# RWKV attention with an ELU feed-forward: one three-bank PSUM tile becomes a two-bank tile and a one-bank tile

## The chip, the cores and the metric

The kernel runs on one core of a Trainium2 chip. The metric is device time in microseconds (us) of one execution. The engines are named as the profile names them: PE is TensorE's matmul side, PEld its weight loads, DVE is VectorE, ACT is ScalarE, POOL is GpSimd, SP is SyncE, whose queue issues nearly all loads.

## The reference

A linear attention with a decaying state, followed by a feed-forward layer. Everything is float32: 4 batches, 8 heads, 768 steps, head width 48; the feed-forward goes from 384 to 2048 and back.

```python
state = np.zeros((B, H, D, D))
for t in range(S):
    kt, vt, rt, wt = k[:, :, t], v[:, :, t], r[:, :, t], w[:, :, t]
    cur = np.einsum('bhd,bhe->bhde', u[None] * kt, vt)
    y[:, :, t] = np.einsum('bhd,bhde->bhe', rt, state + cur)
    state = wt[:, :, :, None] * state + np.einsum('bhd,bhe->bhde', kt, vt)
...
x = y.transpose(0, 2, 1, 3).reshape(B * S, H * D)
h = x @ w_in
g = np.where(h > 0.0, h, np.exp(np.minimum(h, 0.0)) - 1.0)
return g @ w_out
```

## The kernel before

The 768 steps are cut into 24 attention units. Units 0 to 3 each take one batch's first 128 steps ("whole" units); units 4 to 23 each take 64 steps of two batches. From unit 8 on a unit is "stacked": the inter-chunk and intra-chunk parts of an output share one matmul operand. The feed-forward runs in six chunks of 512 tokens (four units each) over 16 slices f of the inner width.

A unit goes through these steps. DVE scans the decay (`es`, `gs`) and scales k and r with it (`rh`). The diagonal term is made by PE and copied out by ACT in units 0 to 3 (`pd`, `md`), later by DVE, and then spread into a masked matrix `am` (`sp`: ACT in units 0 to 3, DVE in 4 to 7, POOL from 8 on). PE transposes k (`tr`), ACT copies the result out (`kt`). PE makes the scores (`s`), and DVE merges them into `am` under the causal mask (`mk`, lines 625 to 631). PE then makes the unit's outputs and the state update (`v`). ACT rounds the outputs to a high part (`xh`, line 692; in whole units by way of a plain copy `xf`, line 699), DVE makes the low part (`xl`, line 696), and DVE adds the update to the state (`up`, line 704; ACT at line 706 in whole units). In stacked units the step `v` of unit i issues three things in a row on PE: the scores of unit i+1, the state update of unit i, and the outputs of unit i.

In the feed-forward, each slice is nine matmuls into a tile `ph` (`g1`, line 303; three in line 299 while a chunk's weights are still plain float32), two ACT passes (`r1`, `r2`, lines 307 and 310), a DVE pass (`stt`, line 313), a split into high and low by ACT (`gh`, line 317) and DVE (`gl`, line 321), and nine matmuls into three accumulators (`g2`, lines 334 and 331). The weights arrive raw and are converted by ACT and DVE during the first 160 us (lines 719 to 753).

PSUM holds eight banks: three accumulators, two `ph`, and the tile `px` of three banks, made once at line 409 and used for the whole run. Banks 0 and 1 of it take the scores and the state update, and, in units 0 and 2 to 7, the outputs too. Unit 1 borrows two accumulators. Bank 2, reached through `single()` at line 445, takes the diagonal sums, the transposes, the outputs of stacked units (line 672) and a small check. In the last chunk the final output block is summed in two column pieces: columns 0 to 383 in bank 0 of `px` and columns 384 to 511 in bank 2 (lines 902 and 903); DVE adds a partial sum to each (line 348).

A planner in the kernel (`Plan`, with costs, due times and hand-fitted nudges) works out the order of all steps once, and they are emitted in that order: each engine works its own steps strictly in it. The planner takes no account of which tile a PSUM bank belongs to. The waits between engines are not written in the kernel: the framework derives them from which instructions touch which tile. A fixed number of filler matmuls into an accumulator (`warm`) stands ahead of some PE steps of the first 28 us.

Of the kernel before, what the change touches and what calls it, by code (L numbers as in the profile page):

```python
# [8 lines left out]
F32 = mybir.dt.float32  # L9
# [11 lines left out]
P = 128  # L21
# [5 lines left out]
NK = DM // P  # L27
N = B * C
GT = 4
L = C // 2  # L30
# [334 lines left out]
def rwkv_elu_kernel(ctx, tc, wkr, rk, vp, u, uz, gkrw, gv, gu, wraw, out):  # L365
# [16 lines left out]
    ps_a = pool("ps_a", 1, space=PS)  # L382
# [23 lines left out]
    xf = wide[:, 0:NK * N].rearrange("p (k n) -> p k n", k=NK)  # L406
    stack = wide.rearrange("p (s h n) -> p s h n", s=3, h=2)
    ams = cst.tile([P, 2, 2 * NP * C], F32, name="ams")
    px = ps_a.tile([P, 3, N], F32, name="px")
    sv = st[:, :, :, 16:16 + D]  # L410
    units = [dict(c=i // B, i=i, whole=i < B, last=i >= NU - STEP, L=C if i < B else L,
                  b=slice(i, i + 1) if i < B else slice(2 * (i % STEP), 2 * (i % STEP) + 2)) for i in range(NU)]
# [30 lines left out]
        return [px[:, q] for q in range(2)] if u_["whole"] else px[:, 0:2]  # L443

    def single():
        return px[:, 2]

    def spare():
        if not held:
# [73 lines left out]
    def diag_pe(u_):  # L523
        u_["pd"] = pd = single()[:, 0:NS].rearrange("t (p z) -> t p z", p=NP)
        for p in range(NP):
            nc.tensor.matmul(pd[:, p], u_["rkc"][:, p, :], ubd[:, p, :], start=True, stop=True)
# [47 lines left out]
    def job(u_, h, p, x, l, r, **flags):  # L574
        k, j = divmod(3 * p + (0, 1, 1, 2)[x], 4)
        nc.tensor.matmul(u_["py"][32 * j:32 * j + 32, h, k], l, r, **flags)  # L576
# [9 lines left out]
    def transposes(u_):  # L586
        u_["pt"] = pt = single()[:, 0:NP * R2].rearrange("t (p d) -> t p d", p=NP)
        for p in range(NP):
            nc.tensor.transpose(pt[:, p], u_["k"][:, p, :], ident[0:R2, 0:R2])

    def scores(u_, pa, each=False, close=True):
        for p in range(NP):
            for lo in range(0, C, u_["L"]):
                for q in range(2):
                    rs, ts = slice(64 * q, 64 * q + D), slice(lo, lo + u_["L"])
                    nc.tensor.matmul(pa[q][ts, p], u_["k"][rs, p, ts], u_["r"][rs, p, ts], start=each or p == 0, stop=each or (close and p == NP - 1))  # L596

    def halves():
        t = px[:, 0:2, 0:NP * L].rearrange("t q (p s) -> t q p s", p=NP)
        return [t[:, q] for q in range(2)]  # L600
# [40 lines left out]
    def update_part(u_, v, **flags):  # L641
        rows = [slice(0, C)] if u_["whole"] else [slice(L * h, L * h + L) for h in range(2)]
        for p in range(NP):
            for z in range(2):
                lo = 64 * z
                for h, rs in enumerate(rows):
                    nc.tensor.matmul(u_["pu"][lo:lo + D, h, p], u_["kt"][rs, p, lo:lo + D], v[h][rs, P * p + 80 * z:P * p + 80 * z + D],  # L647
                                     **{n: x if isinstance(x, bool) else p == x for n, x in flags.items()})
# [15 lines left out]
    def stacked(u_):  # L664
        i, w = u_["i"], u_["stack"]
        ahead = i + 1 < NU
        if ahead:
            scores(units[i + 1], halves(), close=u_["last"])
        if not u_["last"]:
            u_["pu"] = px[0:R2, 0:2, NP * L:NP * L + NP * D].rearrange("d h (p e) -> d h p e", p=NP)  # L670
            update_part(u_, [w[:, h] for h in range(2)], start=False, stop=NP - 1)
        u_["py"] = px[:, 2, 0:2 * NK * L].rearrange("d (h k t) -> d h k t", h=2, k=NK)
        for h in range(2):
            rs = slice(0, P if h else R2)
            for n, (p, x) in enumerate(VALUES):
                job(u_, h, p, x, w[rs, h, P * p + 32 * x:P * p + 32 * x + 32], u_["am"][rs, h, x // 2, p],
                    start=(h == 0 and n < 4), stop=(h == 1 and n >= len(VALUES) - 4))
# [82 lines left out]
    def guard():  # L760
        units[0]["pf"] = pf = single()[0:1, 0:NU + 1]
        nc.tensor.matmul(pf, ones_c, flags, start=True, stop=True)
# [105 lines left out]
    for c in range(NC):  # L868
        fns = mlp(nc, w_h, w_l, ps_acc, ps_h, ml, gp, stg, out[:, c * N:(c + 1) * N], last=c == NC - 1, w_f=() if c else w_f)
        t = BEGINS[c]  # L870
# [244 lines left out]
```

## Time and profile before

| | |
|---|---|
| median of 3 runs | 509.65 us |
| lowest, highest | 508.42, 514.08 us |
| profiled execution, device time | 512.53 us |
| profiled execution, span from first to last instruction | 510.7 us |
| PE busy in the span | 492.8 us (96%) |
| DVE, ACT, POOL busy | 350.3, 271.0, 42.0 us |
| mean granted TensorE clock | 0.990 |

The profiled execution has 1.8 us around its span. Times in the rows below are microseconds from the start of that span. A row of the timeline gives start, duration, engine, line of the kernel, operation, written tile <- read tiles, shape and count, and in brackets how long the engine sat idle before it and what ended that. A tile name has no bank: `px` stands for all three.

### The profile page before, as it was taken

To read this page: it belongs to the slowest core of one execution; us is meant where nothing else is said; L and a number is where in the kernel's file an instruction comes from. 1 tells how busy PE (TensorE), PEld (TensorE's weight loads), DVE (VectorE), ACT (ScalarE), POOL (GpSimd) and SP (SyncE) were. 2 spreads that over 40 slices of the span, in tenths; PEclk is the share of its full clock that TensorE was granted. 3 is DMA by queue.
4 is the path that set the end of the run, shared out by engine and by line. 5 is a ranking of instruction groups with operands and counts; after the bars stand their busy time and mean duration, and the time that the engine had idled before them with its cause. 6 is when DMAs were issued, how large, how long until landed. Compare 5 with 4: busy or idle time off the path is not lost.

```text
span 510.7 us, 12038 instructions
## 1 busy us (share of the span) xinstructions
PE 492.8 (96%) x5014; PEld 404.7 (79%) x5014; DVE 350.3 (69%) x525; ACT 271.0 (53%) x526; POOL 42.0 (8%) x57
## 2 busy tenths in 40 slices
PE   8997999999999999998999999999999999999994
PEld 8896887777887888886887777877888878888883
DVE  7899899989998998544898554599564352323432
ACT  4796568755764544635655525437445253634451
POOL 2000000002234011020011020020101000000000
PEclk9898999999999999999999999999999999999998
DMA  8999246734625444433951427033340100010001
GB/s 280 336 270 286 69 142 198 231 115 125 183 49 125 130 117 104 125 91 88 238 154 53 138 64 195 21 103 84 95 109 11 24 2 0 20 45 0 1 0 65
DMA packets 45611, 57.27 MB, mean 112 GB/s; under 512 B 29168, under 2 KB 29296, under 8 KB 45552
## 3 DMA queue, kind: packets, MB, share of 16 engines
q1 hardware_dynamic: 45120, 55.66, 39.0%
q8 instruction: 41, 0.67, 0.6%
q10 hardware_dynamic: 432, 0.79, 0.4%
q14 instruction: 18, 0.15, 0.1%
HBM read 45.42 MB, written 4.72 MB: 98 GB/s over the span
## 4 chain that ended last, share of the span: by engine, by line
PE 67%; DVE 17%; DMA 7%; issue 3%; ACT 3%; SPq 2%; DVEq 0%; ACTq 0%
PE ph L303 27%; PE acc L334 25%; PE px L576 3%; PE acc L331 3%; PE ph L299 3%; DMA wx<-in_wkr_dram 3%; DMA wraw<-in_wraw_dram 2%; DVE m L313 2%; DVE gl L321 2%; DVE k L502 2%; DVE eg L487 2%; DMA k<-in_wkr_dram 2%; PE px L596 2%; DVE ams L631 1%; PE px L647 1%
## 5 line engine op out<-in xcount | busy, mean ns | idle before, releaser
L313 DVE SCALAR_TENSOR_TENSOR m<-m,ph 128x512 f32<-128x512 f32 (+2 forms) x104 | 66.5, 641 | 72.0 <-ACT m L310 71.9
L303 PE MATMUL ph<-xh,w_l 128*128 128x512 f32 x270 | 105.5, 391 | 0.8 <-DVE w_l L753 0.8
L334 PE MATMUL acc<-gh,w_l 128*128 128x512 f32 x268 | 104.6, 390 | 0.0
L307 ACT ACTIVATE m<-ph 128x512 f32<-128x512 f32 (+2 forms) x104 | 58.5, 563 | 78.8 <-PE ph L303 60.0
L321 DVE TENSOR_TENSOR gl<-m,gh 128x512 fp32r<-128x512 f32 x90 | 62.1, 691 | 41.5 <-ACT gh L317 41.4
L317 ACT CAST gh<-m 128x512 fp32r<-128x512 f32 x90 | 55.5, 617 | 59.4 <-PE acc L334 36.6
L303 PE MATMUL ph<-xh,w_h 128*128 128x512 f32 x180 | 72.2, 401 | 1.5 <-DVE m L313 1.4
L334 PE MATMUL acc<-gl,w_h 128*128 128x512 f32 x180 | 70.6, 392 | 1.4 <-DVE gl L321 1.4
L334 PE MATMUL acc<-gh,w_h 128*128 128x512 f32 x180 | 71.7, 398 | 0.0
L303 PE MATMUL ph<-xl,w_h 128*128 128x512 f32 x180 | 70.2, 390 | 0.0
L310 ACT ACTIVATE m<-m 128x512 f32<-128x512 f32 (+2 forms) x104 | 62.1, 599 | 2.1
L303 PEld LDWEIGHTS ph<-xh,w_l 128*128 128x128 f32 x270 | 50.7, 188 | 12.1 <-DVE w_l L753 1.2
L334 PEld LDWEIGHTS acc<-gh,w_l 128*128 128x128 f32 x268 | 50.3, 188 | 10.3
L555 POOL TENSOR_SCALAR_AFFINE_SELECT ams<-md 64x512 f32<-64x512 f32 x32 | 29.1, 909 | 217.8 <-PE px L576 145.5
L303 PEld LDWEIGHTS ph<-xh,w_h 128*128 128x128 f32 x180 | 33.8, 188 | 9.7 <-DVE m L313 2.1
L334 PEld LDWEIGHTS acc<-gl,w_h 128*128 128x128 f32 x180 | 33.8, 188 | 9.6 <-DVE gl L321 3.1
L334 PEld LDWEIGHTS acc<-gh,w_h 128*128 128x128 f32 x180 | 33.8, 188 | 8.0 <-ACT gh L317 0.4
L303 PEld LDWEIGHTS ph<-xl,w_h 128*128 128x128 f32 x180 | 33.8, 188 | 6.5
L303 PE MATMUL ph<-xh,w_g 128*128 128x512 f32 x90 | 35.6, 395 | 0.1
L334 PE MATMUL acc<-gh,w_g 128*128 128x512 f32 x88 | 34.9, 397 | 0.7 <-ACT gh L317 0.7
L487 DVE TENSOR_TENSOR_SCAN eg<-w,reset 112x520 f32<-112x520 f32 (+1 forms) x24 | 30.7, 1278 | 6.6 <-DMA w<-in_wkr_dram 6.6
L303 PE MATMUL ph<-xl,w_g 128*128 128x512 f32 x90 | 35.1, 390 | 0.0
(110 smaller groups left out, 691.9 us busy)
## 6 DMA issues: line engine op xcount, KB each, us to landing
wraw<-in_wraw_dram SPq DMA_DIRECT2D x16, 768.0 KB, 10.1
k<-in_wkr_dram SPq DMA_DIRECT2D x24, 448.0 KB, 5.4
rk<-in_rk_dram SPq DMA_DIRECT2D x20, 384.0 KB, 4.4
w<-in_wkr_dram SPq DMA_DIRECT2D x24, 227.9 KB, 3.9
wide<-in_vp_dram SPq DMA_DIRECT2D x32, 128.0 KB, 3.5
out_dram<-o SPq DMA_DIRECT2D x15, 256.0 KB, 2.5
ams<-k SPq DMA_DIRECT2D x64, 48.0 KB, 2.6
wide<-st SPq DMA_DIRECT2D x64, 48.0 KB, 2.1
```

The costliest lines, as they stand in the source:

```text
L299: nc.tensor.matmul(ph, w_f[f][:, 0, k], x_[2][:, k], start=(k == 0), stop=(k == NK - 1))
L303: nc.tensor.matmul(ph, w[f][:, 0, k], y[:, k], start=(k == n == 0), stop=(k == NK - 1 and n == 2))
L307: act(s["m"], s["ph"], AF.Relu, scale=-1.0)
L310: act(s["m"], s["m"], AF.Exp, scale=-1.0)
L313: stt_(s["m"], s["m"], -1.0, s["ph"], ALU.add, ALU.max)
L317: nc.scalar.copy(s["gh"], s["m"])
L321: nc.vector.tensor_tensor(s["gl"], s["m"], s["gh"].bitcast(F32), ALU.subtract)
L331: nc.tensor.matmul(a_, w_f[f][:, 1, m], fold(s, s["m"][:, a:b]), start=first, stop=final)
L334: nc.tensor.matmul(a_, w[f][:, 1, m], fold(s, g[:, a:b]), start=(first and n == 0), stop=(final and n == 2))
L487: nc.vector.tensor_tensor_scan(out=eg[:, 0, 0:n][:, ::-1], data0=u_["w"][:, 1:n + 1][:, ::-1], data1=reset[:, 0, 0:n][:, ::-1], initial=0. ...
L555: nc.gpsimd.affine_select(out=am[rs, h].rearrange("t q p s -> t (q p) s"), in_=u_["md"][rs].rearrange("t q p -> t (q p)").unsqueeze(2).bro ...
L576: nc.tensor.matmul(u_["py"][32 * j:32 * j + 32, h, k], l, r, **flags)
```

## The change

The tile of three banks is made as two tiles: `px` with banks 0 and 1, `py` with one bank. What used `px[:, 2]` uses `py`. No step, shape, operand order or planner entry is different.

```diff
-    px = ps_a.tile([P, 3, N], F32, name="px")
+    px = ps_a.tile([P, 2, N], F32, name="px")
+    py = ps_a.tile([P, N], F32, name="py")
...
     def single():
-        return px[:, 2]
+        return py
...
-        u_["py"] = px[:, 2, 0:2 * NK * L].rearrange("d (h k t) -> d h k t", h=2, k=NK)
+        u_["py"] = py[:, 0:2 * NK * L].rearrange("d (h k t) -> d h k t", h=2, k=NK)
```

## Rows read from the trace of the kernel before

**Rows 1.** The page: busy time of the engines, and the chain that ended last.

```profile
PE 492.8 (96%) x5014; PEld 404.7 (79%) x5014; DVE 350.3 (69%) x525; ACT 271.0 (53%) x526; POOL 42.0 (8%) x57
...
PE 67%; DVE 17%; DMA 7%; issue 3%; ACT 3%; SPq 2%; DVEq 0%; ACTq 0%
```

**Rows 2.** Busy time by stretch: stretch, length, then each engine's busy time.

```profile
108.01:153.58 45.57, 44.58 (x646) 35.71 (x645) 45.34 (x66) 27.61 (x54) 11.76 (x11) 1.00 0.43 120
32.64:44.32 11.68, 10.45 (x109) 8.72 (x107) 11.64 (x17) 9.27 (x25) 1.07 (x2) 1.00 1.04 267
```

**Rows 3.** Timeline, PE: instructions before which PE sat idle.

```profile
14.44 1.05 PE L526 MATMUL px<-ubd,rkc 112*128 112x2 f32 x8 [1.22 <-ACT kt L635]
...
46.16 1.76 PE L576 MATMUL px<-ams,wide 128*32 128x128 f32 x32 [2.46 <-issue]
...
102.56 0.60 PE L589 MATMUL px<-ident,k 112*128 112x112 f32 x4 [0.37 <-DVE xl L696]
...
119.42 0.50 PE L303 MATMUL ph<-xh,w_l 128*128 128x512 f32 x1 [0.79 <-DVE w_l L753]
...
163.06 0.50 PE L303 MATMUL ph<-xh,w_h 128*128 128x512 f32 x1 [1.01 <-DVE m L313]
...
232.84 0.50 PE L334 MATMUL acc<-gl,w_h 128*128 128x512 f32 x1 [1.09 <-DVE gl L321]
...
270.15 0.51 PE L334 MATMUL acc<-gh,w_g 128*128 128x512 f32 x1 [0.69 <-ACT gh L317]
```

**Rows 4.** Waits: engine, line <- what ended them: total us, times, longest.

```profile
ACT xh L692 <- DVE ams L631: 25.0, 8, 6.8
...
DVE ams L631 <- PE px L576: 14.3, 5, 4.7
```

**Rows 5.** Timeline, 149 to 155 us: after the outputs of unit 8.

```profile
149.85 1.12 PE L576 MATMUL px<-ams,wide 112*32 112x64 f32 x64
...
152.09 1.49 DVE L631 COPY_PREDICATED ams<-upper_h,px 64x512 f32<-64x512 uint32 x2
...
153.67 0.48 ACT L692 CAST xh<-px 128x384 fp32r<-128x384 f32 x1 [1.60 <-DVE ams L631]
...
154.18 0.55 DVE L704 TENSOR_TENSOR st<-st,px 112x384 f32<-112x384 f32 x1 [0.60 <-ACT xh L692]
```

**Rows 6.** Timeline, 13 to 46 us, ACT and DVE around units 0, 2 and 3.

```profile
13.85 0.53 ACT L635 COPY kt<-px 128x448 f32<-128x448 f32 x1 [1.34 <-DVE ams L625]
...
32.64 1.35 DVE L625 COPY_PREDICATED ams<-upper,px 128x512 f32<-128x512 uint32 x2 [0.42 <-ACT kt L635]
...
42.54 0.71 ACT L310 ACTIVATE m<-m 128x256 f32<-128x256 f32 x2
...
43.91 0.41 DVE L313 SCALAR_TENSOR_TENSOR m<-m,ph 128x256 f32<-128x256 f32 x1
44.72 1.34 DVE L625 COPY_PREDICATED ams<-upper,px 128x512 f32<-128x512 uint32 x2 [0.39 <-ACT kt L635]
```

**Rows 7.** Timeline, DVE, 93 to 109 us.

```profile
93.85 0.75 DVE L627 COPY_PREDICATED ams<-upper_h,px 128x512 f32<-128x512 uint32 x1 [0.94 <-ACT kt L635]
...
108.01 0.96 DVE L753 TENSOR_TENSOR w_l<-wg,w_h 128x768 fp32r<-128x768 f32 x1 [2.08 <-ACT w_h L741]
```

**Rows 8.** Timeline from 502.9 us, then the chain's piece at 504.02.

```profile
502.96 0.34 PE L334 MATMUL px<-gh,w_l 128*128 128x384 f32 x1
...
504.02 0.76 DVE L348 TENSOR_TENSOR o<-px,part 128x384 f32<-128x384 f32 x2 [1.06 <-PE px L334]
...
504.02 0.56 DVE o L348
```

**Rows 9.** The chain that ended last, at 225 us.

```profile
225.78 3.49 DMA wx<-in_wkr_dram
```

**Rows 10.** Waits of PEld at the scores; timeline, PE, outputs of unit 9.

```profile
PEld px L596 <- issue: 4.6, 13, 0.4
...
160.95 1.10 PE L576 MATMUL px<-ams,wide 112*32 112x64 f32 x64
```

## The prediction

> **What bounds the kernel now.** I read the page first: PE is busy 492.8 of 510.7 us, and the chain that ended last runs through PE for 67% and DVE for 17% [rows 1]. So only what shortens PE's idle time, or the end after PE's last matmul, can shorten the run. Then PE's own timeline, for the instructions with idle time ahead of them [rows 3]. Seven such gaps carry most of it: 1.22 us at 14.44, 2.46 at 46.16, 0.37 at 102.56, 0.79 at 119.42, 1.01 at 163.06, 1.09 at 232.84 and 0.69 at 270.15; together 7.6 us, the most that a change of waits could return inside the span. Then who made PE wait: up to 163 us it is DVE or ACT each time. DVE is the second bound there: busy 45.34 of the 45.57 us from 108.01 to 153.58, and 11.64 of 11.68 from 32.64 to 44.32 [rows 2]. In such a stretch a piece of DVE idle time that goes away moves everything behind it.
>
> Last, the accesses to `px` themselves. After the outputs of unit 8 (PE, to 150.97) the mask step on DVE reads banks 0 and 1 from 152.09 to 153.58; the cast on ACT, which reads only the outputs in bank 2, starts at 153.67, 0.09 after the mask's end, having idled 1.60 us; and DVE's state update, banks 0 and 1 again, starts 0.03 after the cast's end (154.15), having idled 0.60 [rows 5]. The reader is to see that two reads of different banks, neither needing the other's result, take turns. The view of waits counts eight such waits of the cast for the mask, 25.0 us in all, and five of the mask for the output matmuls (L576), 14.3 us [rows 4]. In stacked units those write bank 2 alone, which the mask doesn't read. So the order is kept per tile, not per bank, and two tiles should end the turn-taking between bank 2 and the others.
>
> The Trainium skill, "PSUM — Partial Sum Buffer", section "PSUM bank collisions raise a hardware error", asks only for accesses to one bank and quadrant to be kept apart, and reports different banks as running clean together. By that page a guard per bank would do, and were the kernel guarded so already, the split would be worth nothing; the rows of the cast and the mask show a wider guard.
>
> **The change part by part.** It adds no instruction and moves none: order and shapes are the same. It takes waits away. I follow each place where one can reach PE or the end.
>
> *Unit 3, PE at 46.16.* PE waits for the mask that starts at 44.72. DVE idled 0.39 us for the copy of the transposes (bank 2), so that goes. Before the mask stands the DVE step at 43.91, which needs the ACT step that ends at 42.54 + 0.71 = 43.25 [rows 6]; allowing 0.06 for the handover it can start 0.60 earlier, if DVE is ahead by so much. DVE is full from 32.64 on [rows 2], and at 32.64 it idled 0.42, again for the copy of the transposes; further up, the copy at 13.85 idled 1.34 for the mask (banks 0 and 1), and PE 1.22 behind it at 14.44 [rows 3, 6]. So up to 1.64 us of lead come in, and the ACT step at 42.54 lets 0.60 through unless it moves too. I take 0.60 + 0.39 = 1.0 us; the bounds are 0.39 (only the last wait goes) and 1.22 + 0.42 + 0.39 = 2.0. What is late next at 46.16 is the mask itself, no longer the copy. PE's gap of 2.46 has room for all of it. The loads in this stretch keep the 16 DMA engines at a share of 1.04 [rows 2], so steps that wait for data won't come earlier; that is why I stay near the middle.
>
> *Unit 5, DVE at 93.85.* The mask idled 0.94 us for the copy of the transposes. Its scores are ready before, so it starts 0.94 earlier. At 108.01 DVE waits again, 2.08 us for ACT's weight cast [rows 7]; the chain of waits leads from there back to a raw weight load that starts when DVE is done with the buffer, so that wait moves along. I take 0.94; the bounds are 0 (the load lands no earlier) and 0.94.
>
> *Unit 8, DVE at 154.18.* The 0.60 us goes, since the cast can run beside the mask [rows 5]. Behind it DVE works without a break up to the step that releases PE at 163.06. I take 0.60; bounds 0 and 0.60.
>
> These two lead to 1.54 us on DVE, and PE can cash them where it waits for DVE: 0.37 + 0.79 + 1.01 = 2.17 us at 102.56, 119.42 and 163.06 [rows 3]. The gap at 102.56 is itself a wait of the transposes (bank 2) for a read of banks 0 and 1.
>
> *After 163 us.* The gap at 232.84 hangs on ACT's flag steps, which wait for loads that the SP queue issues one after the other after PE's outputs of unit 12; the chain of waits shows one of these loads from 225.78, 3.49 us long [rows 9]. This chain starts at PE and contains no `px` wait that goes, so the gap moves with PE and keeps its size. The one at 270.15 waits for ACT, which is behind the same flag steps. Nearly all of the 25.0 us of ACT and much of the 14.3 us of DVE [rows 4] lie between such gaps, in stretches where PE has work queued, and are worth nothing. I count 0; the bounds are 0 and 1.09 + 0.69 = 1.8.
>
> *The end.* The last block is summed in two column pieces. The first is complete at 502.96 + 0.34 = 503.30, but DVE's two additions start only at 504.02, after the last matmul into bank 2; the first takes 0.56 of the 0.76 us [rows 8]. With two tiles it starts at about 503.41 and is over before the second piece is ready, so the end comes 0.56 earlier, and the last store with it. Bounds 0 and 0.56; nothing covers this, it is the end of the chain.
>
> *What it may cost.* In a stacked unit the first scores carry one wait for everything on `px`; with two tiles the outputs and the transposes need a wait of their own. The nearest rows are PEld's idle time before the scores, 4.6 us in 13 times, 0.35 each, and the outputs of unit 9, which start at 160.95 without idle time although they already depend on the mask and on copied rows [rows 10]. I take 0; the bounds are 0 and 16 x 0.35 = 5.6 us.
>
> Sum: 1.0 + 0.94 + 0.60 + 0.56 = 3.1 us; bounds 0.39 + 0.56 = 0.95 and 2.0 + 0.94 + 0.60 + 0.56 = 4.1.
>
> **The rivals.**
>
> *Nothing happens.* The waits stem from something else that the two steps share, or the framework keeps order by bank, and the split leaves every semaphore as it is. For it: the trace names tiles, not banks, and releasers are inferred. Against it: the cast starts 0.09 after the mask in unit 8 and is released by the mask eight times. The page's rule on banks, if followed by the program, leads here too. Time: unchanged, 512.5 in the profiled execution, 509.65 as a median.
>
> *The later gaps close too.* ACT gets 25.0 us of idle time back and DVE starts its masks up to 1.1 us earlier (the outputs' length, 1.10 [rows 10]), so that the flag steps and the splits behind them reach PE in time. Then 4.1 + 1.8 = 5.9 us: 506.6, or 503.7 as a median. Against it: the load at 225.78.
>
> *Slower: PE waits twice.* Each of the 16 stacked units gets a stop between update and outputs. At 0.35 us each that is 5.6 us, less the 3.1: 515.0, or 512.2 as a median. It decides once a stop costs more than 3.1 / 16 = 0.19 us. Against it: the outputs' start at 160.95 [rows 10], at a place where PE has to observe other engines already.
>
> **How the numbers follow.** The profiled execution took 512.53 us, 1.8 around its span of 510.7. With 3.1 us less that is 509.4 (span 507.6). The median of the runs shown is 509.65, 2.9 lower than the profiled one; I carry the difference over: 509.65 - 3.1 = 506.6. Chances: this forecast 0.60, nothing 0.21, later gaps 0.11, PE waits twice 0.08. The forecast's own range is 505.5 to 508.7. The lowest run lay 1.2 us under its median, which brings the low end to 504.3, a little lower for the larger gain; the high end takes in "nothing", 509.65, and half as much scatter again as below, since the runs go 4.4 us above their median: 504.0 to 510.6. One per cent, 5.1 us, is about what a measurement of this kernel can tell from no change. Faster by more than that takes the larger gain (most of 0.11) or a lucky tail of the forecast: 0.12. Slower by more than 5.1 us takes twice-waiting at more than its price or a disturbed median: 0.04. Within 1%: 0.84.
>
> **What would show it.** Right: the cast at L692 and the mask at L631 overlap in time; the wait of the cast for the mask (25.0 us) is gone from the view of waits; the mask in stacked units starts after the update matmuls, about 1.1 us before the outputs end; the first PE gap at 14.44 is gone and that at 46.16 starts about 1 us earlier; no DVE idle time at the masks of units 2, 3 and 5; PE's gap at 163 is smaller and comes about 2.5 us earlier; the gaps near 232 and 270 keep their size; the first of the two last additions starts before PE's last matmul ends. Wrong: the cast still follows the mask (nothing happens); a new idle time of PE between L647 and L576 (it waits twice); or the leads of unit 3 and unit 5 are lost at DVE's wait near 108, because the weight load lands when it did.

## The result, and the profile after

The changed kernel takes 503.47 us as the median of nine executions (501.96 to 509.25), beside 511.0 us (508.31 to 514.08) for nine of the kernel before on the same chip: a ratio of 0.9878, with a 95% interval of 0.9833 to 0.9922. That is 1.2% less; the forecast of 3.1 us is 0.6%. Applied to the 509.65 us that the forecast started from, the ratio gives 503.4 us, just under the low end of the stated range (504.0). The profiled execution took 502.57 us with a span of 500.9 us, 9.8 us less than the profiled one of before.

The page of the changed kernel: busy times, and the chain that ended last by engine (before: [rows 1]).

```profile
PE 488.9 (98%) x5014; PEld 403.0 (80%) x5014; DVE 350.0 (70%) x525; ACT 270.6 (54%) x526; POOL 41.4 (8%) x57
...
PE 62%; DVE 18%; DMA 10%; issue 4%; ACT 3%; SPq 2%; DVEq 0%; ACTq 0%
```

PE lost 3.9 us of busy time with the same 5014 matmuls, which a removed wait alone can't do. So the two profiles differ in PE's speed as well as in its idle time. The timeline of the changed kernel around unit 8 and at the end (before: [rows 5, 8]; line numbers are one higher, and `py` is the split-off bank):

```profile
147.01 0.47 ACT L693 CAST xh<-py 128x384 fp32r<-128x384 f32 x1
147.12 1.50 DVE L632 COPY_PREDICATED ams<-upper_h,px 64x512 f32<-64x512 uint32 x2
...
148.65 0.56 DVE L705 TENSOR_TENSOR st<-st,px 112x384 f32<-112x384 f32 x1
...
496.51 0.56 DVE L348 TENSOR_TENSOR o<-px,part 128x384 f32<-128x384 f32 x1 [0.45 <-PE px L334]
...
496.75 0.27 PE L334 MATMUL py<-gh,w_l 128*128 128x128 f32 x1
497.06 0.29 DVE L348 TENSOR_TENSOR o<-py,part 128x128 f32<-128x128 f32 x1
```

The cast of `py` and the mask out of `px` now run side by side, the state update follows the mask without idle time, and the first of the two last additions starts before PE's last matmul. The view of waits of the changed kernel (before: [rows 4, 10]):

```profile
ACT xh L693 <- PE py L577: 14.9, 9, 5.2
DVE ams L632 <- PE px L648: 7.1, 2, 3.6
PEld px L597 <- issue: 5.3, 15, 0.4
```

The casts' 25.0 us of waiting for the mask are gone; what is left of their waiting is for their own outputs. PEld's idle time at the scores hardly changes (4.6 to 5.3 us), and no output matmul of a stacked unit has PE idle ahead of it, so no second stop was added. PE's timeline of the changed kernel, at the places of [rows 3]:

```profile
13.20 1.05 PE L527 MATMUL py<-ubd,rkc 112*128 112x2 f32 x8
...
42.60 1.08 PE L577 MATMUL px<-ams,wide 128*32 128x128 f32 x32 [2.27 <-ACT kt L636]
...
97.79 0.69 PE L597 MATMUL px<-k 48*64 48x64 f32 x32 [0.21 <-DVE xl L697]
...
114.44 0.50 PE L303 MATMUL ph<-xh,w_l 128*128 128x512 f32 x1 [0.82 <-DVE w_l L754]
...
157.52 0.50 PE L303 MATMUL ph<-xh,w_h 128*128 128x512 f32 x1 [0.40 <-DVE m L313]
...
263.89 0.47 PE L334 MATMUL acc<-gh,w_g 128*128 128x512 f32 x1
```

The gap at 14.44 is gone (but see experiment 12: a late load had made most of it), the one at 46.16 keeps 2.27 us and comes 3.6 us earlier, the one at 163.06 has gone from 1.01 to 0.40 us, and that at 270.15, which was to keep its size, is closed. The one at 232.84 stayed (1.23 us, at 227.19), and so did the wait for `w_l` (0.79 at 119.42, now 0.82 at 114.44).

The lead over the profile of before holds more than waits. At unit 3 it is 3.6 us, of which 0.7 was there from the start: the mask of unit 0, which waits for a load of `k`, begins at 11.76 and not at 12.44. By 50 us it is 5.1: before, the 32 matmuls at 46.16 took 1.76 us; here the same ones take 1.08 [rows 3]. In the profiled execution of before PE was granted half its clock (1.2 of 2.4 GHz) in two stretches of the first 50 us, each right behind one of the first two large gaps; in the one after, nowhere ahead of PE's last matmul. Two windows of the profile of before (columns: stretch, length, busy time of PE, PEld, DVE, ACT and POOL with the number of instructions, granted clock, DMA share, GB/s):

```profile
16.00:18.00 2.00, 2.00 (x12) 1.94 (x10) 1.97 (x3) 1.97 (x9) 0.00 (x0) 0.50 1.02 290
48.00:50.00 2.00, 2.00 (x20) 1.70 (x21) 2.00 (x4) 1.14 (x4) 0.00 (x0) 0.55 0.99 245
```

The executions of one kernel differ in this too: the nine of the changed kernel have a mean granted clock between 0.986 and 1.000, and the longest of them has the lowest. So executions have to be compared at equal clock. Over 169 executions of all kernels below, fitted with one slope and a level for each kernel, 0.01 of mean clock goes with 4.8 us. "At full clock" below is a time less this share; ± is one standard error. The ratios leave out eight slow executions (over 1.5% above the fastest of their kernel); left out of the last column too, they move experiment 3 to -2.7 and every other row by 0.3 us or less.

| kernel | runs | median us | ratio to before (95%) | mean clock | at full clock, against before on the same chip |
|---|---|---|---|---|---|
| changed | 9 | 503.47 | 0.988 (0.983 to 0.992) | 0.9947 | about -5.1 ± 0.8 |
| 1 all waits back | 12 | 509.60 | 0.998 (0.994 to 1.002) | 0.9917 | -0.1 ± 0.3 |
| 2 units 0 to 3 back | 8 | 505.02 | 0.991 (0.988 to 0.995) | 0.9965 | -3.1 ± 0.5 |
| 3 units 4 to 23 back | 12 | 507.23 | 0.993 (0.989 to 0.996) | 0.9942 | -2.0 ± 0.5 |
| 4 tail in one tile | 8 | 505.02 | 0.990 (0.986 to 0.994) | 0.9955 | -3.5 ± 0.6 |
| 5 units 4 to 7 back | 6 | 502.48 | 0.986 (0.982 to 0.989) | 0.9978 | -5.4 ± 0.7 |
| 6 units 8 to 23 back | 6 | 505.46 | 0.990 (0.987 to 0.994) | 0.9977 | -3.0 ± 0.6 |
| 7 ACT's waits back | 6 | 503.65 | 0.988 (0.984 to 0.993) | 0.9957 | -5.0 ± 0.6 |
| 8 PE's waits back | 6 | 505.64 | 0.990 (0.986 to 0.995) | 0.9952 | -4.3 ± 0.8 |
| 9 DVE's waits back | 6 | 505.62 | 0.990 (0.986 to 0.993) | 0.9935 | -4.9 ± 0.4 |
| 10 gap filled | 6 | 503.20 | 0.987 (0.984 to 0.989) | 0.9975 | -5.0 ± 0.6 |
| 11 mask first | 6 | 504.07 | 0.988 (0.985 to 0.991) | 0.9988 | -3.5 ± 0.3 |
| 12 before, tail apart | 12 | 509.41 | 0.997 (0.994 to 1.001) | 0.9938 | -1.4 ± 0.5 |

For the changed kernel the clock of the executions of before beside it was not recorded; their mean of 510.9 us is taken down by 3.7 us, for the mean clock of 0.9923 that 66 other executions of before have. So of the 6.2 us between the means, 510.9 and 504.7, about 5.1 are left at equal clock and 1.1 are clock.

### The profile page after: what moved, and what is told of

The parts are those of the page before. It is cut to its first block, busy times and chain, and to the rows that moved or that the text cites. A ratio compares the mean times of both kernels' runs of the same rounds, so it can differ in the third digit from the quotient of the medians.

```text
span 500.9 us, 12029 instructions
## 1 busy us (share of the span) xinstructions
PE 488.9 (98%) x5014; PEld 403.0 (80%) x5014; DVE 350.0 (70%) x525; ACT 270.6 (54%) x526; POOL 41.4 (8%) x57
## 4 chain that ended last, share of the span: by engine, by line
PE 62%; DVE 18%; DMA 10%; issue 4%; ACT 3%; SPq 2%; DVEq 0%; ACTq 0%
PE ph L303 27%; PE acc L334 25%; DMA wraw<-in_wraw_dram 5%; DMA wx<-in_wkr_dram 3%; PE acc L331 2%; DMA k<-in_wkr_dram 2%; DVE gl L321 2%; DVE m L313 2%; PE py L577 2%; DVE k L503 2%; PE ph L299 2%; DVE eg L488 2%; DVE ams L632 1%; PE px L597 1%; DVE w_l L754 1%
## 5 line engine op out<-in xcount | busy, mean ns | idle before, releaser
L334 PE MATMUL acc<-gl,w_g 128*128 128x512 f32 x88 | 34.6, 393 | 0.2
```

The costliest lines, as they stand in the source:

```text
L334: nc.tensor.matmul(a_, w[f][:, 1, m], fold(s, g[:, a:b]), start=(first and n == 0), stop=(final and n == 2))
```

## The experiments

My theory when I began was that the gain beyond the forecast was earned in the first 50 us, by the two gaps there and the half clock behind them. The rivals: it came from the later, stacked units, or the clock is chance.

### 1 to 3: the waits put back, all, early or late

The two tiles stay, and each step on them is made to wait for the last step of every other engine on either, as the tracker did for the one tile. The order and the kinds of waits are then those of the kernel before, apart from the tail. In the cut below `BACK` stands for each run's condition, and the lines that skip steps on other banks are not shown.

```diff
+        tie_last = {}
         for t in plan.order():
...
+            tie_a = len(tie_insts())
             t["fn"]()
+            tie_made, tie_key = tie_insts()[tie_a:], t["key"]
+            if tie_key[0] in ("pd", "md", "s", "tr", "kt", "mk", "v", "xf", "xh", "xl", "up"):
...
+                if BACK:   # 1: True; 2: tie_i < 4; 3: tie_i >= 4; 5: 4 <= tie_i < 8; 6: tie_i >= 8
+                           # 7 to 9: t["eng"] == "ACT", "PE", "DVE"
+                    for tie_e, tie_x in tie_last.items():
+                        if tie_e != t["eng"]:
+                            tc.add_manual_dep(tie_made[0], tie_x.name, tie_sync, reason="tie")
+                tie_last[t["eng"]] = tie_made[-1]
```

> Two tiles as in the changed kernel, but each step that touched the single tile waits by hand for the last step of every other engine on it, as the tracker made it wait before. All theories: a control. The median within 0.4% of before (509 to 513 us), and in the profile PE again idles about 1.2 us ahead of unit 1's diagonal sums and about 2.4 us ahead of unit 3's outputs, and the mask is again what releases ACT's casts. The tail alone keeps its separate bank (0.6 us ahead of before). If it is as fast as the changed kernel, the gain comes from where the tiles lie and not from waits, and all theories fall.

> The same waits by hand, but only in units 0 to 3 (the first 50 us); from unit 4 on the changed kernel's. Theory (most of the gain is earned in the first 50 us: two PE gaps that shrink, and the half clock that followed each of them): 508 to 509.5 us, only 1.5 to 2.5 us under before, PE idles 1.2 and 2.4 us ahead of unit 1's diagonal sums and unit 3's outputs, and the granted clock is near 0.5 behind at least one of the two gaps. Rival (what was gained beyond the forecast lies in the later, stacked units): 505 us, close to the changed kernel. Rival (the half clock is chance, and comes with or without the waits): the two gaps are back (2.4 us lost, 506 us) but the clock after them is as full as in the changed kernel.

> The same waits by hand, but only from unit 4 on; units 0 to 3 as in the changed kernel. Theory (early): 504.5 to 506 us, 1 to 2 us over the changed kernel: unit 5's gap at about 98 us, unit 8's at 157 us and the one near 264 us are each some 0.3 to 0.6 us longer, and there is no half clock in the first 50 us. Rival (later units): 508 to 510 us.

With all waits back the time is that of before: -0.1 ± 0.3 us at full clock. The view of waits with all waits back has the cast behind the mask again, and the mask behind the outputs:

```profile
ACT xh L693 <- DVE ams L632: 28.2, 9, 6.8
...
DVE ams L632 <- PE py L577: 14.2, 5, 4.6
```

So the gain is in the waits and not in where the tiles lie. One thing does not add up: this kernel keeps the tail apart, which experiment 12 prices at 1.4 ± 0.5 us, and isn't that much faster than before. Waits set by hand may be a little stricter than the tracker's own.

My theory, that the early waits hold most of the gain, fell. They cost 2.0 us at full clock (-5.1 to -3.1), the late ones 3.1 (-5.1 to -2.0); which of the two costs more is within the errors of about 0.9. And the early gaps were back without the half clock. PE's timeline with only the early waits back, then two windows of it:

```profile
14.39 1.05 PE L527 MATMUL py<-ubd,rkc 112*128 112x2 f32 x8 [1.24 <-ACT kt L636]
...
45.82 1.08 PE L577 MATMUL px<-ams,wide 128*32 128x128 f32 x32 [2.45 <-issue]
```

```profile
46.00:48.00 2.00, 2.00 (x51) 1.70 (x44) 1.97 (x4) 0.56 (x2) 0.00 (x0) 1.00 1.02 394
48.00:50.00 2.00, 2.00 (x11) 1.77 (x10) 2.00 (x5) 0.92 (x3) 0.00 (x0) 1.00 1.02 235
```

Here PE idled 2.45 us and ran at full clock behind it. With all waits back, the same gap (2.46 us ahead of 46.52) was followed by half clock:

```profile
46.00:48.00 2.00, 1.48 (x29) 1.51 (x32) 1.97 (x4) 0.63 (x1) 0.00 (x0) 0.50 1.00 333
48.00:50.00 2.00, 2.00 (x29) 1.44 (x19) 2.00 (x4) 0.69 (x3) 0.00 (x0) 0.50 1.02 381
```

The two profiles also show how a lead is given away. Both the changed kernel and the one with early waits back ran at full clock up to PE's last matmul. At unit 3 the latter is 3.2 us behind (45.82 against 42.60), at PE's wait for the weight conversion, 114.44 in the changed kernel, 2.0 us, behind the gap at 227.19 1.3 us, and at PE's last matmul 0.94 us. These are two single executions: in experiment 2 the mask of unit 0 starts 0.6 us later for a late load of `k`, and experiment 5, which has more waits than the changed kernel, reaches PE's last matmul 1.4 us ahead of it, at full clock too.

### 5 and 6: which of the late waits

> Waits by hand in units 4 to 7 alone. So far, with every execution brought to full granted clock by the common slope (0.01 of mean clock is 4.75 us), before stands at 506.3, the changed kernel at 502.2, all waits back at 506.3, early ones at 503.2, late ones at 504.3. Theory 1 (what the late waits cost is unit 5's, as the prediction's second term has it, 0.9 us): 503.1 at full clock, and in the profile PE idles about 1.5 us ahead of unit 5's transposes (97 to 100 us) as with all late waits, of which some 1.2 us is given back at 114 us. Theory 2 (it is the stacked units'): 502.3, and the idle time at 97 to 100 us is under 0.4 us.

> Waits by hand from unit 8 on, units 0 to 7 as in the changed kernel. Theory 1: about 503 at full clock (unit 8's 0.6 us and little after it), PE's gaps near 157 and 264 us longer by 0.3 to 0.7 us each. Theory 2 (the stacked units hold the late gain): 504.3 at full clock, as with all late waits.

The waits of units 4 to 7 show no cost (-5.4 ± 0.7 against -5.1 ± 0.8, errors that don't by themselves exclude the forecast's 0.94), though the gap ahead of unit 5's transposes is back; from unit 8 on they cost 2.1 us (-3.0 ± 0.6). PE's timeline with the waits of units 4 to 7 back:

```profile
97.59 0.57 PE L590 MATMUL py<-ident,k 112*128 112x112 f32 x4 [0.95 <-ACT gh L317]
```

Experiment 6 runs the changed kernel's waits up to unit 7 and shows what this lead is worth. Its PE is at these transposes 1.0 us earlier (96.58), but then waits 0.46 us for DVE's `xl` and 0.35 us ahead of the outputs, and comes to the next feed-forward products at 99.24, where experiment 5 is at 99.10. The lead is gone within 3 us. DVE had given it away before: in experiment 6 it waits 0.90 us at 93.57 for ACT, in the changed kernel at three steps:

```profile
90.38 0.96 DVE L735 SCALAR_TENSOR_TENSOR wg<-wg,wraw 128x768 uint32<-128x768 uint32 x1 [0.44 <-ACT wraw L725]
...
93.77 0.96 DVE L735 SCALAR_TENSOR_TENSOR wg<-wg,wraw 128x768 uint32<-128x768 uint32 x1 [0.20 <-ACT wg L720]
94.92 0.69 DVE L313 SCALAR_TENSOR_TENSOR m<-m,ph 128x512 f32<-128x512 f32 x1 [0.19 <-ACT m L310]
```

In the kernel before, DVE had no idle time at these three (95.89, 98.81, 99.67). Now it waits there for ACT, whose part of the weight conversion waits for raw weight loads (1.29 us at 88.23, 0.64 at 92.02). PE's later wait for `w_l` is another matter: it stands in two of the fourteen profiles, that of before and that of the changed kernel. The raw weight load ahead of it took 6.6 and 6.9 us there, 4.6 to 6.0 in the others but for experiment 7 (6.6).

With the waits from unit 8 on back (experiment 6), two gaps are larger than in the changed kernel (0.40 and none):

```profile
156.92 0.50 PE L303 MATMUL ph<-xh,w_h 128*128 128x512 f32 x1 [0.96 <-DVE m L313]
...
264.53 0.50 PE L334 MATMUL acc<-gh,w_g 128*128 128x512 f32 x1 [0.81 <-ACT gh L317]
```

The first is unit 8's term. The second was counted at nothing; with 0.31 us right behind it, it puts PE back by 1.3 us against the changed kernel. The chain behind it, in the kernel with the waits from unit 8 on, and then in the changed one:

```profile
258.42 4.18 DMA wx<-in_wkr_dram
262.63 0.03 ACT wx L507
...
263.45 0.53 ACT m L310
264.00 0.55 DVE m L313
```

```profile
258.90 2.82 DMA wx<-in_wkr_dram
261.75 0.03 ACT wx L507
...
262.57 0.53 ACT m L310
263.13 0.55 DVE m L313
```

The load is issued 0.5 us earlier and lands 0.9 us later. In all fourteen profiles this last `wx` load takes 4.1 to 4.6 us where the waits of PE from unit 8 on stand (before, 1, 3, 6, 8, 12), and 2.7 to 3.0 us where they don't, but for experiment 11 (3.8). The SP queue issues the same transfers in the same order ahead of it in both, so which of them it shares the engines with when, and why that costs 1.4 us, was not settled.

A third place has no gap in PE's rows, since ends of matmuls are modelled: around 302 us PE loses another 0.5 us against the changed kernel. Experiment 6, then the mask there in the changed kernel:

```profile
298.49 1.50 DVE L632 COPY_PREDICATED ams<-upper_h,px 64x512 f32<-64x512 uint32 x2 [4.60 <-PE py L577]
...
302.86 0.19 PEld L334 LDWEIGHTS acc<-gl,w_h 128*128 128x128 f32 x1 [0.45 <-DVE gl L321]
```

```profile
296.65 1.52 DVE L632 COPY_PREDICATED ams<-upper_h,px 64x512 f32<-64x512 uint32 x2 [3.51 <-PE px L648]
```

With the waits the mask starts behind the outputs (L577), without them behind the update (L648), and the split `gl` that PE's weights wait for comes behind the mask. The three places make 2.3 us in this pair of profiles, where the times give 2.1.

### 7 to 9: by the engine that waits

> Waits by hand in all units, but only those in which ScalarE's step waits (the casts and copies out of the output bank wait for the mask and the update again; TensorE and VectorE don't wait by hand). Theory (what costs is ScalarE waiting for VectorE's mask): most of the gain is gone, 505 to 506 at full clock, and the mask is the releaser of the casts for 25 us or more. Rival (TensorE's own waits, a write to one bank behind a reader of the other): 502.2 to 503.0 at full clock.

> Waits by hand in all units, but only those in which TensorE's step waits (transposes, scores, outputs and diagonal sums wait for the last VectorE and ScalarE step on either tile). Theory (ScalarE's waits cost): 502.2 to 503.2 at full clock and the casts wait for TensorE's outputs, not for the mask. Rival (TensorE's own waits): 505 to 506, with PE's gap of 1.2 us ahead of unit 1's diagonal sums back in either case, since there the mask holds TensorE directly if not through the copy.

> Waits by hand in all units, but only those in which VectorE's step waits (the mask and the update wait for TensorE's outputs and for ScalarE's copies on either tile). So far, at full clock: waits of ScalarE alone 501.9, of TensorE alone 502.7, the changed kernel 502.1, all waits 506.1. Theory 1 (the loss from unit 8 on, 1.9 us, is the stacked mask waiting for the outputs of the unit before, which the list of waits shows 5 times for 14.2 us with those waits back and not with TensorE's alone): 503.5 to 504.2 at full clock, and PE's gap at 157 us is 0.9 us. Theory 2 (no kind costs by itself, since each chain finds its way round one kind): 502 to 502.8, and the gap at 157 us stays at 0.4 us.

No kind shows a cost by itself: -5.0, -4.3 and -4.9 at full clock, each within its error (0.9 to 1.1) of the changed kernel, while all three together cost 5.0. ACT's wait for the mask is back in experiment 7:

```profile
ACT xh L693 <- DVE ams L632: 25.6, 9, 5.8
```

It is worth nothing that the times show. The likely reason is that the cost needs waits on both sides: a step held up on one engine holds up the next engine's step on another bank, and so on round, while with one kind left the other two engines run on and the held one catches up in its own idle time. That is argued and not shown: no run put back two kinds of the three.

### 4 and 12: the tail

The call alone is shown, cut out of its line.

```diff
-  rest(x, y, b, single, "b")
+  rest(x, y, b, lambda: px[:, 1], "b")                                        # 4, changed kernel
+  rest(x, y, b, lambda: ps_h.tile([P, N], F32, tag="ph", name="ph"), "b")     # 12, kernel before
```

> The changed kernel, but the last two column pieces of the output lie in one tile again (the two score banks), so the first addition waits for the second piece's products. All theories: 0.3 to 0.6 us over the changed kernel, below what times can tell; in the profile the first of the two last additions starts 0.56 us later against the products' own times, and nothing else moves. How long the last store takes from issue to landing (4.56 us in the profile before, 2.10 us in the one after) tells whether that follows the kernel or the run: 2.1 us here if it follows the earlier additions, any value if it is chance.

> The kernel before with its lasting three-bank tile, and one thing of the change alone: the last 128 columns of the output are summed in a tile of their own (one of the two hidden-layer banks, free by then), so the first of the last two additions no longer waits for their products. The fourth term of the sum, 0.56 us: 506.0 at full clock against 506.6 of before, 509.5 to 510 median, the first addition starts before the last six products end, and the last store is issued about 1.3 us after the one before it in place of 1.8 us. Theory 1 (the last store also lands sooner then: 4.56 and 3.19 us with the pieces in one tile, 2.10 to 2.92 us in the eleven profiles with them apart): it lands in 2.1 to 2.9 us and the time is 505.0 at full clock. Theory 2 (its landing is chance): 3 us or more is as likely here.

Both ways the tail comes out above 0.56 us at full clock, 1.6 ± 1.0 in the changed kernel and 1.4 ± 0.5 in the one before, though neither error excludes 0.56. The view of the line that stores the result, for the three stores of before, then of before with the tail apart:

```profile
L352 ACTq DMA_DIRECT2D out_dram<-o x3: 339/381/1108, 502.2 to 504.8; - x3
...
DMA to landing us min/median/max: 2.9/3.1/4.6
```

```profile
L352 ACTq DMA_DIRECT2D out_dram<-o x3: 339/382/1067, 499.2 to 501.3; - x3
...
DMA to landing us min/median/max: 2.7/2.8/3.0
```

The last store is issued 1.3 us behind the one ahead of it and not 1.8, which is the 0.5 us of the forecast. It also lands sooner: in 2.10 to 2.92 us in the twelve profiles with the pieces apart, 3.19 and 4.56 us in the two with them together (which are the two longest of fourteen; by chance that is 1 in 91). Why a store issued half a microsecond earlier lands faster is not known.

### 10 and 11: the gap at unit 3

The first comment stands for the lines that move steps in the order.

```diff
+  # 10: ("kt", 3) behind ("s", 3); 11: also ("mk", 3) behind it, ("es", 4) and ("pc", 4) behind ("stt", 5)
+  for _ in range(n if t["key"] == ("v", 3) else 0):   # n = 7 in 10, 4 in 11
+      nc.tensor.matmul(single()[:, 0:P], ones, ones, start=True, stop=True)
```

> The changed kernel with unit 3's transposed keys copied out right after its scores and 7 filler products (1.8 us at full clock) written to the output bank ahead of unit 3's outputs, where TensorE idles 2.0 to 2.5 us in every run so far. No work is moved. Theory 1 (the half-clock stretches follow gaps of TensorE, above all this one: 5 of the 10 profiles show one within 1.5 us of its end): none at 41 to 50 us here, mean granted clock 0.997 or more over the executions against 0.995 of the changed kernel, median 501.5 to 502.5. Theory 2 (they come and go with something else): mean clock 0.995 and 503.5 to 505, with a half-clock stretch near 45 us as likely as before.

> As the kernel with the gap filled, and unit 3's mask moved ahead of unit 4's first scan and of both products behind it on VectorE, with 4 fillers in place of 7. Unit 3's outputs start 0.8 to 1.2 us earlier, the gap with its fillers is 1.2 to 1.5 us. If that lead reaches the end: 501 at full clock (1.1 us under the changed kernel). If, as with unit 5's lead, a later wait for VectorE's weight conversion (114 us) or unit 8's takes it back: 502, no change.

PE's timeline with the gap filled:

```profile
40.18 1.83 PE L985 MATMUL py<-ones 128*128 128x128 f32 x14
42.39 1.08 PE L577 MATMUL px<-ams,wide 128*32 128x128 f32 x32 [0.38 <-DVE ams L626]
```

Neither profile has half clock ahead of the end, and the mean clock is 0.9975 and 0.9988. But experiments 5 and 6, with unit 3's gap of 1.96 us in place, have 0.9978 and 0.9977, so the high clock can't be put down to the filling. The median (503.20) misses the 501.5 to 502.5 that I expected and can't be told from the changed kernel's. With the mask first, unit 3's outputs start 0.7 us earlier, and PE then waits 1.33 us at 50.17 for a step that DVE does later; at full clock it is 1.6 ± 0.9 us slower than the changed kernel. No version here beats that one by more than the error.

## Why the prediction was right, and where its sizes were off

The mechanism was right: the tracker tied banks together that share no data, cast and mask now overlap, the casts' 25 us of waits are gone, the additions at the end start early, no second stop appeared at the scores. That the casts' 25 us would be worth next to nothing by themselves was right too (experiment 7). One sign is weaker than it looked: the first gap is gone, but most of its 1.22 us came from a late load of `k`, as experiment 12 shows with the waits in place. Its unit 1 and its unit 3:

```profile
13.32 1.05 PE L526 MATMUL px<-ubd,rkc 112*128 112x2 f32 x8 [0.18 <-ACT kt L635]
...
44.33 1.08 PE L576 MATMUL px<-ams,wide 128*32 128x128 f32 x32 [2.46 <-issue]
```

The size was not right: 3.1 us were forecast and 5.1 ± 0.8 came at equal clock, 6.2 with the clock. I had given 0.12 to a gain over 1%; the measured 1.2% has an interval from 0.8 to 1.7%. Term by term:

- *Unit 3, 1.0 us: too small.* The waits of units 0 to 3 are worth 2.0 ± 0.9 us at full clock. At unit 3 the changed kernel is 1.7 us ahead of experiment 12 and 3.2 ahead of experiment 2; the load of `k` at the start takes 0.5 off the one and adds 0.6 to the other.
- *Unit 5, 0.94 us: no gain is seen* (experiment 5), the lower bound. The step that failed is "a piece of DVE idle time that goes away moves everything behind it", and with it "I take 0.94": DVE loses the lead between 90 and 95 us, at waits for the weight conversion and its raw loads, which before were over when DVE came. The prediction looked for such a wait at 108 us only. That wait did move along (to 103.02, 1.87 us).
- *Unit 8, 0.60 us: right.* 0.56 us in the gap at 157.
- *After 163 us, counted 0.* This step failed, and it is the largest miss. The gap at 270.15 did not keep its size: it closes with the 0.31 us behind it, because the load behind ACT's flag step lands in 2.8 and not in 4.3 us. PE's lead over before grows there from 5.35 to 6.50 us, so the place is worth 1.15, within the bound of 1.8; another 0.5 comes at 302 us, from the earlier mask. That the gap at 232.84 keeps its size was right. The rival "the later gaps close too" gave 503.7 us; the time came out there, but the 1.09 us at 232.84 that it counted did not close, the gap that did was closed by a load, and only the 0.5 us at 302 came in its way.
- *The end, 0.56 us: too small.* The additions gave 0.5 us, and the last store's landing some 0.3 to 2.5 us more, which no row of before could show; by the times the whole is 1.4 ± 0.5.
- *The clock.* The sum had no term for it. 1.1 us of the 6.2 are a higher mean clock.

Added up by the times at full clock: 2.0 for units 0 to 3, -0.3 for 4 to 7, 2.1 from 8 on and 1.6 for the tail are 5.4 of the 5.1 ± 0.8 us. One pair of profiles without half clock ahead of the end agrees, experiment 12 and the changed kernel: PE's lead is 1.73 us at unit 3 and 2.14 at 113.00, falls to 1.15 behind the wait for `w_l`, is 1.45 behind unit 8, 3.41 at 264.47 and 3.87 at PE's last matmul, without the tail, which both have. The errors are large enough that a missing part of 1 us would not be seen.

My first reading of the two profiles, that the extra gain was the first 50 us and their half clock, was wrong, though it fitted all their rows: 3.8 of the 9.8 us between the two spans are clock in that pair (0.990 against 0.998, at 4.8 us for 0.01), and the rest mixes a `k` load that DVE waited 1.17 us for before (0.61 in the changed kernel, none in experiment 12) with the waits.

## What to carry to other kernels

One buffer for several banks lets the tracker tie engines together that share no data; how long the engines wait for it says little of what it costs, which has to be measured by putting parts back. Before a lead at one place is counted, follow it past the next waits of the bounding engine: those that hang on something else, here raw weight loads and their conversion, take it back. Compare executions at equal granted clock, for a pair of profiles with unlike clock can support a wrong story in all its rows.

## What the runs showed of the hardware

TensorE's clock fell to half behind idle time of PE of one to two and a half microseconds, but not each time. Unit 3's gap of 1.96 to 2.46 us stands in twelve profiles and half clock follows, or sets in during it, in six of them; where it was 0.4 us (10 and 11), in neither. The gap near 100 us ahead of unit 5's transposes or scores was followed by half clock in all four profiles where it was 1.36 to 1.67 us (1, 3, 7, 8) and in none of the ten where it was under 1 us. Gaps of 1.60 us (experiment 1, at 14.79) and 1.33 us (experiment 11, at 50.17) were followed by none. Before the half clock PE had in each case been idle; the length of the idle time alone doesn't decide it. The kernels with waits on every engine (before and experiment 1) have a mean clock of 0.992 over 78 executions, the changed kernel and all others that build on it 0.996 over 79. With errors of 0.0004 on either mean, part of the higher clock goes with the removed waits; which gaps did it is not shown. The Trainium skill, "TensorE: Matmul & The Clock Gate", section "What's actually happening", calls the clock's rise at a kernel's start "run-variable". No run here shows that rise, since the granted clock is 1.00 over the first 14 us of all fourteen profiles; what varies here between executions of one kernel is the mean clock (0.986 to 1.000).

With the two banks in tiles of their own, ACT read one while DVE read the others (147.01 and 147.12 above) and both took as long as before, within 0.01 us (0.47 and 1.50 against 0.48 and 1.49 us, [rows 5]).
